# One four-bank score tile and one exp per chunk in a sliding-window attention kernel

## The chip, the cores and the metric

The kernel runs on one core of one Trainium2 chip. The metric is device time in microseconds (us). An execution mostly repeats within 0.3% to 1%.

Names of engines: PE is the tensor engine (PEld its weight loads), ACT the scalar engine, DVE the vector engine, POOL the general-purpose engine, SP the engine that issues most transfers. PSUM has eight banks of 512 fp32 columns per partition (the Trainium skill, "PSUM — Partial Sum Buffer", Specifications), and the pools of this kernel take exactly eight.

## The reference, cut to what matters

```python
x = A_x                                          # 2048 tokens, 512 features, bf16
h = layernorm(x) * (1 + ca) + sa
q, k, v = split(h @ wqkv)                        # 32 heads of 16
scores = q @ k.T * 16**-0.5                      # causal, window of 256
x = x + ga * (softmax(masked scores) @ v @ wo)
h = layernorm(x) * (1 + cb) + sb
x = x + gb * token_mlp(layernorm(h))             # over tokens: 2048 -> 1792, gelu, -> 2048
```

The modulation vectors `ga`, `ca` and so on come from a small product with `w_mod`.

## The kernel before

The queries are worked off in 4 groups of 512 tokens, each with 4 head groups of 8 heads. A head group of query group 0 has four chunks and every other has five, 76 in all. A chunk is up to 512 score columns for each of four row tiles (32 rows of the array each, two heads to a row tile). It goes PE (scores) to ACT (exp) to DVE (two mask multiplications) to PE (attention-value, AV, and the sum of the exps). Projections of the next query group, output projections, layer norms and the first part of the MLP are cut into slices and emitted between chunks as background.

Four of the eight banks hold scores, as two tiles of two banks. Two banks serve the background (`ps_d`) and two the AV results (`ps_o`), so all eight are taken.

```python
ps_d = ...tile_pool(name="ps_d", bufs=2, space=PSUM)
ps_s = ...tile_pool(name="ps_s", bufs=2, space=PSUM)    # two tiles of two banks
ps_o = ...tile_pool(name="ps_o", bufs=1, space=PSUM)

def emit_scores(G, g8, ch):
    tiles = []
    for a in range(2):
        pss = ps_s.tile([P, 2, D], F32, name="pss")
        for kb, qs, nq, col in ch:
            ...
            for jj in range(2):
                rows = slice(32 * (2 * a + jj), 32 * (2 * a + jj) + 32)
                nc.tensor.matmul(pss[:, jj, col : col + KB * nq], ..., tile_position=(32 * (2 * a + jj), 0))
        tiles.append(pss)
    return tiles

def emit_exp_mask(tiles, ch, masks):
    et = epool.tile([P, 4, D], BF, name="et")
    for a in range(2):
        nc.scalar.activation(out=et[:, 2 * a : 2 * a + 2, lo:D], in_=tiles[a][:, :, lo:D], func=ACT.Exp, scale=SCORE_SCALE)
    for col, stride, m0, mn in masks:            # two multiplications on DVE
        ...

for i, (u, ci, ch, mk) in enumerate(steps):
    ...
    et = emit_exp_mask(tiles, ch, mk)            # exp and masks of chunk i
    tiles = emit_scores(... steps[i + 1] ...)    # scores of chunk i + 1
    pend.append((u, ci, ch, et))
    ...                                          # slices of background
    emit_av(...)                                 # AV of chunk i - 1; after the last chunk Ln, Exp, normalise
```

After attention the score banks serve the MLP as accumulators, two output blocks to a tile. The framework tracks a PSUM tile as a whole.

The softmax here doesn't subtract the row's maximum and nothing guards it: scores larger than these inputs give would overflow.

## Time and profile before

| | before |
|---|---|
| time, median | 318.3 us |
| profiled span | 316.3 us |
| first exp starts / last exp ends | 23.3 / 225.4 us |
| that stretch | 202.1 us, 2.66 us a chunk |
| after the last exp | 90.9 us |

The page of the kernel before gives busy time and share of the span by engine (first two rows), and the chain that ended last by engine (third):

```profile
PE 266.9 (84%) x3271; PEld 130.4 (41%) x3313; DVE 229.4 (73%) x517; ACT 184.2 (58%) x241; POOL 33.8 (11%) x68
...
PE 45%; ACT 20%; DVE 19%; issue 5%; another core or an unknown queue 0%
```

No engine reads as full, and the chain runs through three of them.

The groups of instructions by form (line, engine, operation, out<-in, shape, count, then busy us and mean ns, then idle time before them and what ended it) give the two lengths of an exp:

```profile
L417 ACT ACTIVATE et<-pss 128x1024 bf16<-128x1024 f32 x144 | 140.7, 1033 | 26.8 <-PE pss L403 26.4
...
L417 ACT ACTIVATE et<-pss 128x768 bf16<-128x768 f32 x8 | 6.2, 819 | 6.5 <-PE pss L403 6.5
```

The timeline of ACT (start, length, what) holds this row:

```profile
89.84 5.81 ACT L417 ACTIVATE et<-pss 128x1024 bf16<-128x1024 f32 x6
```

Six exps take 5.81 us, about 0.97 each; where one directly follows another, starts are 0.904 us apart (median of 72). Finally, from the waits of PE (who waited on whom: us in total, times, longest):

```profile
PE pss L403 <- ACT et L417: 9.6, 27, 0.7
...
PE poy L469 <- DVE et L424: 2.4, 1, 2.4
```

Scores wait for an exp a little each time, and AV hardly ever waits for a mask. Three rows of PE's timeline show the usual order of its work here, scores, then a slice of background (`pv`), then AV:

```profile
89.11 0.85 PE L403 MATMUL pss<-QT_1_128,KT_1_136 32*128 32x128 bf16 x12
89.89 1.06 PE L326 MATMUL pv<-wqkv,h1T 128*64 128x256 bf16 x16
90.89 0.27 PE L469 MATMUL pox<-et,VT_144 128*32 128x192 bf16 x4
```

### The profile page before, as it was taken

How to read it: one execution, taken by the hardware profiler on the slowest of the kernel's cores; microseconds unless marked ns; L12 is line 12 of the kernel's file. 1: busy time of each engine (PE TensorE's matmuls, PEld its weight loads, DVE VectorE, ACT ScalarE, POOL GpSimd, SP SyncE). 2: the span in 40 equal slices, each digit the busy share in tenths (PEclk: the TensorE clock that was granted, in tenths of full speed). 3: DMA queues.
4: the chain of work that ended last, by engine and by line, in shares of the span. 5: the costliest groups of instructions: out<-in, count | busy, mean ns of one | idle time of the engine just before them, and what ended most of it. 6: DMA issues, size and time to landing. Idle time of an engine off the chain costs nothing.

```text
span 316.3 us, 7673 instructions
## 1 busy us (share of the span) xinstructions
PE 266.9 (84%) x3271; PEld 130.4 (41%) x3313; DVE 229.4 (73%) x517; ACT 184.2 (58%) x241; POOL 33.8 (11%) x68
## 2 busy tenths in 40 slices
PE   0488898988895989988699898899992999999994
PEld 0343345434453534445244444444441444444441
DVE  7989998656999865999774498945389376455353
ACT  2016887799895799899496699977511254000000
POOL 8501301121020032020041000000000000000000
PEclk9999999999998699999699999999999899999999
DMA  7993007900000000000001300033310895101111
GB/s 215 335 349 34 3 2 200 264 6 2 2 3 2 2 2 2 2 2 3 1 2 51 86 2 2 0 105 99 93 42 0 289 414 227 52 34 50 50 35 51
DMA packets 31435, 24.63 MB, mean 78 GB/s; under 512 B 6056, under 2 KB 29608, under 8 KB 31400
## 3 DMA queue, kind: packets, MB, share of 16 engines
q1 hardware_dynamic: 30336, 23.08, 23.9%
q10 hardware_dynamic: 1064, 1.05, 1.1%
q8 instruction: 26, 0.43, 0.6%
q14 instruction: 9, 0.07, 0.1%
HBM read 22.03 MB, written 2.10 MB: 76 GB/s over the span
## 4 chain that ended last, share of the span: by engine, by line
PE 45%; ACT 20%; DVE 19%; issue 5%; another core or an unknown queue 0%
ACT et L417 15%; PE pu L446 6%; PE pss L403 5%; DVE st L243 4%; PE pox L469 4%; PE poy L469 2%; ACT lz L481 2%; PE pu_4759 L653 2%; PE pu_4917 L653 2%; PE pu_4798 L653 2%; PE pu_4956 L653 2%; PE pq L291 2%; PE pv L326 2%; DVE et L424 2%; ACT lz L480 1%
## 5 line engine op out<-in xcount | busy, mean ns | idle before, releaser
L417 ACT ACTIVATE et<-pss 128x1024 bf16<-128x1024 f32 (+1 forms) x152 | 146.8, 1022 | 33.3 <-PE pss L403 32.9
L469 PE MATMUL poy<-et,ones_bd 128*32 128x128 bf16 (+4 forms) x768 | 42.4, 257 | 2.6 <-DVE et L424 2.4
L424 DVE TENSOR_TENSOR et<-et,maskt 128x256 bf16<-128x256 bf16 (+2 forms) x104 | 35.4, 360 | 12.3 <-ACT et L417 12.0
L429 DVE TENSOR_TENSOR et<-et,maskt 128x512 bf16<-128x512 bf16 x48 | 21.2, 442 | 18.0 <-ACT et L417 17.4
L653 PEld LDWEIGHTS <-w2r 128*128 128x128 bf16 x224 | 21.9, 98 | 26.5
L469 PE MATMUL pox<-et,VT_143 128*32 128x320 bf16 (+4 forms) x352 | 19.4, 259 | 3.5 <-DVE OT_1_151 L482 1.2
L469 PEld LDWEIGHTS <-ones_bd 128*32 128x32 bf16 x768 | 19.5, 98 | 6.7 <-issue 4.5
L291 PE MATMUL pq<-h1T,wqkv 128*128 128x512 bf16 x58 | 17.1, 401 | 3.0 <-DVE VT_143 L336 1.3
L326 PE MATMUL pv<-wqkv,h1T 128*64 128x256 bf16 x256 | 18.6, 285 | 0.6 <-DVE KT_0_131 L306 0.5
L300 PE MATMUL pk<-h1T,wqkv 128*128 128x512 bf16 x57 | 16.5, 397 | 2.2 <-DVE kb L312 0.9
L621 ACT ACTIVATE g<-a,b1FM 128x512 bf16<-128x512 f32 x14 | 9.6, 716 | 12.4 <-DVE a L619 12.4
L326 PEld LDWEIGHTS <-h1T 128*64 128x64 bf16 x256 | 13.3, 113 | 4.7 <-issue 2.6
L469 PEld LDWEIGHTS <-VT_143 128*32 128x32 bf16 x352 | 9.1, 96 | 13.5 <-issue 12.9
L246 ACT ACTIVATE rs<-mv,eps_t 128x4 f32<-128x4 f32 x12 | 3.7, 307 | 18.7 <-DVE mv L244 18.7
L312 DVE CAST kb<-pk 128x512 bf16<-128x512 f32 x15 | 10.3, 688 | 5.6 <-issue 2.5
L469 PE MATMUL pox<-et,VT_144 128*32 128x320 bf16 (+4 forms) x208 | 11.1, 268 | 2.5 <-DVE OT_1_147 L482 2.1
L480 ACT ACTIVATE lz<-poy 128x512 f32<-128x512 f32 x16 | 9.7, 608 | 4.4 <-PE poy L469 4.3
L469 PE MATMUL pox<-et,VT_145 128*32 128x320 bf16 (+4 forms) x208 | 11.1, 261 | 1.0 <-DVE OT_2_152 L482 0.5
L336 DVE CAST VT_143<-pv 64x512 bf16<-64x512 f32 x16 | 11.0, 687 | 0.2
L481 ACT ACTIVATE lz<-lz 128x512 f32<-128x512 f32 x16 | 10.4, 649 | 0.0
L300 PEld LDWEIGHTS <-wqkv 128*128 128x128 bf16 x64 | 5.5, 101 | 9.5 <-issue 4.7
L291 PEld LDWEIGHTS <-wqkv 128*128 128x128 bf16 x64 | 5.5, 100 | 8.5 <-issue 3.6
(647 smaller groups left out, 547.3 us busy)
## 6 DMA issues: line engine op xcount, KB each, us to landing
w2r<-in_B_w_dram SPq DMA_DIRECT2D x14, 512.0 KB, 10.0
wmod<-in_w_mod_dram SPq DMA_DIRECT2D x4, 512.0 KB, 6.9
out_dram<-otile SPq DMA_DIRECT2D x16, 128.0 KB, 1.7
wmod<-in_w_mod_dram ACTq DMA_DIRECT2D x2, 512.0 KB, 5.7
wqkv<-in_A_wqkv_dram SPq DMA_DIRECT2D x2, 384.0 KB, 6.2
wqkv<-in_A_wqkv_dram SPq DMA_DIRECT2D x1, 512.0 KB, 6.6
wod<-in_A_wo_dram SPq DMA_DIRECT2D x1, 512.0 KB, 8.6
w1p_1241<-in_B_w_dram SPq DMA_DIRECT2D x1, 512.0 KB, 4.0
```

Source lines behind the costliest of these rows:

```text
L291: nc.tensor.matmul(pq[:], lhsT=wqkv[:, dc, g8 * P : (g8 + 1) * P], rhs=h1T[:, dc, :], start=(dc == 0), stop=(dc == ND - 1),)
L300: nc.tensor.matmul(pk[:], lhsT=wqkv[:, dc, D + g8 * P : D + (g8 + 1) * P], rhs=h1T[:, dc, :], start=(dc == 0), stop=(dc == ND - 1),)
L326: nc.tensor.matmul(pv[KB * par : KB * (par + 1), i, :].rearrange("p (a d) -> p a d", d=DH), lhsT=h1T[:, dc, tok], rhs=wv[:, dc, par, :, :] ...
L403: nc.tensor.matmul(pss[:, jj, col : col + KB * nq], lhsT=KT[r][g8][rows, kbi, :, :], rhs=QT[G % 2][g8][rows, KB * qs : KB * (qs + nq)], st ...
L417: nc.scalar.activation(out=et[:, 2 * a : 2 * a + 2, lo:D], in_=tiles[a][:, :, lo:D], func=ACT.Exp, scale=SCORE_SCALE,)
L424: nc.vector.tensor_tensor(out=dst, in0=dst, in1=msk.to_broadcast([P, 4, KB * mn]), op=ALU.mult,)
L429: nc.vector.tensor_tensor(out=dst, in0=dst, in1=maskt[:, m0 : m0 + 2, :].unsqueeze(1).to_broadcast([P, 4, 2, KB]), op=ALU.mult,)
L446: nc.tensor.matmul(pu[:], lhsT=w1s(sc, fc), rhs=hb[sc][:], start=(sc == 0), stop=(sc == 7),)
L469: nc.tensor.matmul(dst[32 * j : 32 * j + 32, KB * qs : KB * (qs + nq)], lhsT=VT[r][:, kbi, 4 * u.g8 + j, :] if isv else ones_bd[:], rhs=et ...
L480: nc.scalar.activation(out=lz[:], in_=u.y[:], func=ACT.Ln)
L481: nc.scalar.activation(out=lz[:], in_=lz[:], func=ACT.Exp, scale=-1.0)
L653: nc.tensor.matmul(ftiles[100 + t], lhsT=w2r[:, fc, t * P : (t + 1) * P], rhs=guT[fc][:], start=(fc == 0), stop=(fc == NF - 1), skip_group ...
```

## The change

The intent is to halve the number of exps and of score groups, saving their fixed costs. The score tile becomes one tile of four banks. As there are only four banks for it, there is one buffer instead of two. The MLP uses the same pool, so its accumulators follow: four output blocks to one tile.

```diff
-    ps_s = ctx.enter_context(tc.tile_pool(name="ps_s", bufs=2, space=PSUM))
+    ps_s = ctx.enter_context(tc.tile_pool(name="ps_s", bufs=1, space=PSUM))
...
-        for a in range(2):
-            pss = ps_s.tile([P, 2, D], F32, name="pss")
-            for kb, qs, nq, col in ch:
-                for jj in range(2):
+        pss = ps_s.tile([P, 4, D], F32, name="pss")
+        for kb, qs, nq, col in ch:
+            for j in range(4):
                     (the same matmul, row tile j)
...
-        for a in range(2):
-            nc.scalar.activation(
-                out=et[:, 2 * a : 2 * a + 2, lo:D], in_=tiles[a][:, :, lo:D], func=ACT.Exp, scale=SCORE_SCALE,
-            )
+        nc.scalar.activation(
+            out=et[:, :, lo:D], in_=tiles[:, :, lo:D], func=ACT.Exp, scale=SCORE_SCALE,
+        )
...
-    f_tiles([("s", [0, 1]), ("s", [2, 3]), ("x", [4]), ("y", [5])])
+    f_tiles([("s", [0, 1, 2, 3]), ("x", [4]), ("y", [5])])
...
-    homes = [("d", 1), ("d", 1), ("s", 2), ("s", 2), ("x", 1), ("y", 1)]
+    homes = [("d", 1), ("d", 1), ("x", 1), ("y", 1), ("s", 4)]
```

More of the change, by code (lines that the diff above doesn't have):

```diff
@@ L395, in emit_scores @@
     def emit_scores(G, g8, ch):
-        tiles = []
-        for a in range(2):
-            pss = ps_s.tile([P, 2, D], F32, name="pss")
-            for kb, qs, nq, col in ch:
-                r, kbi = ring(kb, G)
-                for jj in range(2):
-                    rows = slice(32 * (2 * a + jj), 32 * (2 * a + jj) + 32)
-                    nc.tensor.matmul(
-                        pss[:, jj, col : col + KB * nq],
-                        lhsT=KT[r][g8][rows, kbi, :, :],
-                        rhs=QT[G % 2][g8][rows, KB * qs : KB * (qs + nq)],
-                        start=True, stop=True, tile_position=(32 * (2 * a + jj), 0),
-                        skip_group_check=True,
-                    )
-            tiles.append(pss)
-        return tiles
+        pss = ps_s.tile([P, 4, D], F32, name="pss")
+        for kb, qs, nq, col in ch:
+            r, kbi = ring(kb, G)
+            for j in range(4):
+                rows = slice(32 * j, 32 * j + 32)
+                nc.tensor.matmul(
+                    pss[:, j, col : col + KB * nq],
+                    lhsT=KT[r][g8][rows, kbi, :, :],
+                    rhs=QT[G % 2][g8][rows, KB * qs : KB * (qs + nq)],
+                    start=True, stop=True, tile_position=(32 * j, 0),
+                    skip_group_check=True,
+                )
+        return pss
     def emit_exp_mask(tiles, ch, masks):
@@ L415, in emit_exp_mask @@
         et = epool.tile([P, 4, D], BF, name="et")
-        for a in range(2):
-            nc.scalar.activation(
-                out=et[:, 2 * a : 2 * a + 2, lo:D], in_=tiles[a][:, :, lo:D], func=ACT.Exp, scale=SCORE_SCALE,
-            )
+        nc.scalar.activation(
+            out=et[:, :, lo:D], in_=tiles[:, :, lo:D], func=ACT.Exp, scale=SCORE_SCALE,
+        )
         for col, stride, m0, mn in masks:
@@ L584, in f_tiles @@
             if kind == "s":
-                t = ps_s.tile([P, 2, D], F32, name="pu2", tag="pss")
+                t = ps_s.tile([P, 4, D], F32, name="pu2", tag="pss")
                 for i, fc in enumerate(group):
@@ L627 @@
         gelu(fc)
-    for kind, group in (("d", [6]), ("d", [7]), ("s", [8, 9]), ("s", [10, 11]), ("x", [12]), ("y", [13])):
+    for kind, group in (("d", [6]), ("d", [7]), ("s", [8, 9, 10, 11]), ("x", [12]), ("y", [13])):
         f_tiles([(kind, group)])
```

## The prediction

> **What bounds the kernel now.** The page: PE busy 84% of 316.3 us, DVE 73%, ACT 58%. Exps run from 23.3 to 225.4 us (timeline), 2.66 us a chunk; there the change acts. By windows, ACT is busy 36.5 of 45.5 us in head group 0 (DVE 39.0), 44.2 of 50.5 in group 1, 45.3 of 54.7 in group 2, 42.6 of 52.0 in group 3 (PE 46.9). No engine is full; the chain of waits gives PE 45%, ACT 20%, DVE 19%. Two score tiles let the next scores fill one while the exp reads the other: six exps run back to back from 89.84 to 95.65 us (timeline).
>
> **Removed.** 76 of 152 exps. A 1024-column exp takes 1.02 us, but back to back their starts are 0.904 us apart. At 0.836 ns per column (groups by form: 819 ns for 768 columns, 1033 for 1024) a 2048-column exp should take 1.88 us (estimate), 4 us less in all. The Trainium skill ("Perfetto Trace Analysis", Optimizing Scalar/DVE Operations) says grouping helps a saturated engine; this trace shows the fixed cost mostly overlapped.
>
> Four row tiles now stand next to each other, not two and two. A chunk's twelve take 0.6 us now, a half group of six 0.40 us. Twelve on four row tiles should take 0.43 us (estimate): 0.17 us of PE per chunk saved, 13 us in all, off the path.
>
> **Added.** One four-bank buffer: the next scores wait for the whole exp, the next exp for all scores. Timeline: exp end to first score 0.05 us, scores 0.43, last score to exp 0.04: 0.52 us with ACT idle. "Perfetto Trace Analysis" (Matmuls) advises rotating banks so that evacuation overlaps the next matmuls; those six exps show that it works here. A chunk's floor becomes 1.88 + 0.52 = 2.40 us instead of 1.81.
>
> **On the critical path.** Twenty chunks of a group: 48 us, plus four normalisation pairs (Ln, Exp; 0.5 us each beyond the gap) and small work: 51 us before any lateness, against 50.5, 54.7 and 52 measured with it. In the built order one attention-value group (AV) and a slice of background, about 1.63 us of PE, stand between two score groups: nearly an exp. AV waits for masks (0.43 + 0.28 us after the exp), so slack is 0.1 to 0.3 us, and late DVE work now delays scores and exp at once. I expect 3 to 8 us more in groups 1, 2 and 3 each, 1 to 3 in group 0 (DVE-bound), 0 to 1 in the MLP tail.
>
> **Prediction: 330 us, range 318 to 344.** Faster by over 2%: 0.06; within 2%: 0.24; slower by over 2%: 0.70.
>
> **What would show each step.**
> - 76 exps, mean about 1.88 us; ACT busy within 4 us of 184.
> - No exp directly after another: ACT idle ended by score matmuls rises from 33 us in 28 waits to over 45 in some 60.
> - Scores wait for the exp far more than 27 times.
> - The exp stretch grows from 202 us to 210 to 218.
> - Time after the last exp changes under 2 us.
>
> **What would make it wrong.** If PE and DVE lateness sets today's 2.66 us rather than ACT, saved PE time and an evener order could hide the 0.52 us: within 2%, or faster. If AV waits long for masks, every chunk slips and it passes 344. If four row tiles don't overlap: +13 us.

## More of the kernel before

The program order is not the issue order: the framework's scheduler orders each engine's queue from its own estimate of when inputs are ready.

The windows of exactly the exp stretch (columns: window, length, then busy time and instruction count of PE, PEld, DVE, ACT, POOL, then granted clock, DMA share, GB/s):

```profile
23.33:225.41 202.08, 176.27 (x2755) 87.70 (x2789) 156.92 (x378) 168.42 (x215) 22.80 (x30) 0.97 0.15 37
```

PE is busy 176.3 of 202.1 us here, so it is idle for 25.8.

Counted over the exp stretch, PE goes from scores to background 69 times and from scores straight to AV 40 times.

## The result, and the profile after

| | before | after |
|---|---|---|
| time, median | 318.31 us | 332.75 us |
| ratio, 95% interval | | 1.0475, 1.042 to 1.053 |
| profiled span | 316.3 us | 329.7 us |
| first exp starts | 23.3 us | 24.7 us |
| exp stretch | 202.1 us | 210.9 us |
| after the last exp | 90.9 us | 94.1 us |

The result is right against the reference. The 13.4 us of span come as 1.3 before the first exp, 8.9 in the exp stretch and 3.2 in the tail. The page after:

```profile
PE 256.8 (78%) x3269; PEld 125.8 (38%) x3313; DVE 227.3 (69%) x517; ACT 182.6 (55%) x165; POOL 34.8 (11%) x68
...
PE 37%; DVE 35%; ACT 15%; DMA 8%; issue 3%; SPq 1%; another core or an unknown queue 0%; DVEq 0%; ACTq 0%
...
L413 ACT ACTIVATE et<-pss 128x2048 bf16<-128x2048 f32 (+1 forms) x76 | 140.6, 1851 | 35.2 <-PE pss L401 34.6
```

There are half as many exps, and together they save little: ACT's busy time on the page falls by 1.6 us. PE does less work (10.1 us less busy) and yet the kernel is longer. The windows of the exp stretch say where:

```profile
24.65:235.59 210.94, 166.55 (x2778) 83.98 (x2815) 154.85 (x376) 166.20 (x137) 23.86 (x30) 0.98 0.15 37
```

PE busy fell from 176.3 to 166.6 us, but PE idle (length less busy) rose from 25.8 to 44.4. The waits of PE after name what it waited for:

```profile
PE pox L465 <- DVE et L425: 13.3, 21, 1.3
...
PE pss L401 <- ACT et L413: 7.0, 14, 1.3
PE pox L465 <- DVE et L420: 3.7, 10, 0.5
PE poy L465 <- DVE et L420: 3.5, 7, 0.9
```

AV now waits 20.5 us for masks (13.3 + 3.7 + 3.5), against 2.4 before. Waits for the exp are no more than before. Six rows of the timeline show the step, ACT's rows first and then PE's (the bracket is the idle time before, and what ended it):

```profile
92.97 1.88 ACT L413 ACTIVATE et<-pss 128x2048 bf16<-128x2048 f32 x1 [0.50 <-PE pss L401]
96.18 1.88 ACT L413 ACTIVATE et<-pss 128x2048 bf16<-128x2048 f32 x1 [1.33 <-PE pss L401]
```

```profile
92.52 0.40 PE L401 MATMUL pss<-QT_1_128,KT_1_136 32*128 32x192 bf16 x8
...
93.81 0.27 PE L465 MATMUL pox<-et,VT_144 128*32 128x192 bf16 x4 [0.88 <-DVE et L425]
...
94.39 1.40 PE L326 MATMUL pv<-wqkv,h1T 128*64 128x256 bf16 x18
95.73 0.40 PE L401 MATMUL pss<-QT_1_128,KT_1_136 32*128 32x128 bf16 x12
```

The exp that started at 92.97 ends at 94.85. Its successor's scores could start then. But PE stood waiting 0.88 us for the masks of the chunk before, does its AV and a slice of background, and reaches the scores only at 95.73. The next exp starts at 96.18, after 1.33 us of ACT idle. The gap before the exp at 92.97 was a turn without lateness, 0.50 us.

The order of PE's work has changed too: AV follows the scores at once, and the background comes after it. PE now goes from scores to background 15 times and straight to AV 62 times (69 and 40 before). The edit did not ask for this. It is the order that the framework's scheduler built for one buffer, and it leaves the masks less time. Why the scheduler chose it is not known.

Counted over all 75 gaps between exps, the medians of the parts are: scores 0.399 us from first start to last end, last score to exp 0.052 us, and in 35 gaps the scores start within 0.07 us of the exp's end. In the other 40 they are late, by 19.0 us in all.

### The profile page after: what moved, and what is told of

Read it like the earlier page. It is cut to its first block, busy times and chain, and to the rows that moved or that the text cites. A ratio compares the mean times of both kernels' runs of the same rounds, so it can differ in the third digit from the quotient of the medians. Undisturbed runs are those within 1.5% of the kernel's fastest.

```text
span 329.7 us, 7582 instructions
## 1 busy us (share of the span) xinstructions
PE 256.8 (78%) x3269; PEld 125.8 (38%) x3313; DVE 227.3 (69%) x517; ACT 182.6 (55%) x165; POOL 34.8 (11%) x68
## 4 chain that ended last, share of the span: by engine, by line
PE 37%; DVE 35%; ACT 15%; DMA 8%; issue 3%; SPq 1%; another core or an unknown queue 0%; DVEq 0%; ACTq 0%
ACT et L413 11%; DVE st L243 6%; PE pu_4802 L649 4%; PE pu_4645 L649 4%; PE pu L442 4%; DVE et L420 4%; PE pss L401 3%; PE pox L465 3%; DVE et L425 3%; PE pu_4257 L592 2%; DMA x_73<-in_A_x_dram 2%; DMA wqkv<-in_A_wqkv_dram 2%; PE pu_4484 L592 2%; DMA b2b<-in_B_b_dram 2%; DVE VT_143 L336 2%
## 5 line engine op out<-in xcount | busy, mean ns | idle before, releaser
L413 ACT ACTIVATE et<-pss 128x2048 bf16<-128x2048 f32 (+1 forms) x76 | 140.6, 1851 | 35.2 <-PE pss L401 34.6
L420 DVE TENSOR_TENSOR et<-et,maskt 128x256 bf16<-128x256 bf16 (+2 forms) x104 | 32.9, 338 | 9.9 <-ACT et L413 9.6
L465 PE MATMUL pox<-et,VT_143 128*32 128x320 bf16 (+4 forms) x352 | 18.4, 255 | 9.3 <-DVE et L425 4.3
L465 PEld LDWEIGHTS <-ones_bd 128*32 128x32 bf16 x768 | 20.4, 97 | 8.3 <-DVE et L420 7.3
L326 PE MATMUL pv<-wqkv,h1T 128*64 128x256 bf16 x256 | 19.3, 277 | 1.1 <-DVE KT_0_131 L306 0.5
L465 PEld LDWEIGHTS <-VT_143 128*32 128x32 bf16 x352 | 11.4, 94 | 17.6 <-issue 16.5
L465 PE MATMUL pox<-et,VT_144 128*32 128x320 bf16 (+4 forms) x208 | 11.3, 264 | 7.3 <-DVE et L425 4.6
L465 PE MATMUL pox<-et,VT_145 128*32 128x320 bf16 (+4 forms) x208 | 10.7, 256 | 6.6 <-DVE et L425 4.3
L312 DVE CAST kb<-pk 128x512 bf16<-128x512 f32 x15 | 10.2, 682 | 5.8 <-PE pk L300 3.0
L465 PEld LDWEIGHTS <-VT_144 128*32 128x32 bf16 x208 | 7.2, 98 | 11.8 <-issue 11.0
L465 PEld LDWEIGHTS <-VT_145 128*32 128x32 bf16 x208 | 6.9, 96 | 10.8 <-issue 9.9
L477 ACT ACTIVATE lz<-lz 128x512 f32<-128x512 f32 x16 | 10.1, 631 | 0.4
```

The source lines that it names most:

```text
L326: nc.tensor.matmul(pv[KB * par : KB * (par + 1), i, :].rearrange("p (a d) -> p a d", d=DH), lhsT=h1T[:, dc, tok], rhs=wv[:, dc, par, :, :] ...
L413: nc.scalar.activation(out=et[:, :, lo:D], in_=tiles[:, :, lo:D], func=ACT.Exp, scale=SCORE_SCALE,)
L420: nc.vector.tensor_tensor(out=dst, in0=dst, in1=msk.to_broadcast([P, 4, KB * mn]), op=ALU.mult,)
L465: nc.tensor.matmul(dst[32 * j : 32 * j + 32, KB * qs : KB * (qs + nq)], lhsT=VT[r][:, kbi, 4 * u.g8 + j, :] if isv else ones_bd[:], rhs=et ...
```

## The experiments

Throttled time will be needed for reading them: the trace records stretches in which PE is granted half its clock. In the exp stretch they come to 13.7 us before and 10.2 us after, so they don't explain the result.

### MLP accumulators as before

The changed attention, with its score pool closed before the MLP and two two-bank tiles opened in its place.

```diff
+    sst.close()
+    ps_s = ctx.enter_context(tc.tile_pool(name="ps_m", bufs=2, space=PSUM))
-                t = ps_s.tile([P, 4, D], F32, name="pu2", tag="pss")
+                t = ps_s.tile([P, 2, D], F32, name="pu2", tag="pss")
     (and the three lists of blocks as before)
```

> The changed kernel, but with the MLP part of the kernel before (two two-bank tiles instead of one four-bank tile; attention is built in the same order). Theory: after the last exp the changed kernel takes 94.1 us against 90.9, because the last four output blocks share one tile and each block's first matmul waits for the vector engine's read of the block before it (about 0.8 us, three times at the end). Then this run loses 2.5 to 3.5 us: about 329.5 us, with 90.5 to 92 us after the last exp, and a start-to-end exp stretch of 211 us as in the changed kernel. Rival: the longer tail comes from the later end of attention itself; then it stays at 332 to 334 us with a tail of 94 us.

Measured: 328.82 us, ratio to before 1.033 (1.025 to 1.041). The stretch stayed at 211.6 us, and the tail fell to 90.0 us. The chain of the changed kernel shows the cause (start, length, what):

```profile
310.24 3.04 PE pu_4802 L649 x14
313.28 0.03 issue
313.30 0.76 DVE o_4817 L632
314.06 0.04 issue
314.10 3.19 PE pu_4802 L649 x14
```

Fourteen matmuls fill one bank of the four-bank tile. The next fourteen go to another bank, but as it is the same tile they wait until DVE has read the first: 0.8 us, three times in the last four blocks. With the accumulators as before, the end of the chain is unbroken PE work:

```profile
299.81 7.12 PE pu L652 x33
306.93 0.05 issue
306.99 10.74 PE pu L652 x49
317.73 0.05 issue
317.78 4.49 PE pu L652 x20
```

The two-bank tiles have the same wait. There the scheduler put matmuls of another tile into it; with the four-bank tile last there was no other. So the 3.2 us by which the tail had grown belong to the MLP and not to attention: undoing the MLP part took 4.1 us off the tail, 3.1 off the span and 3.9 off the median (different rounds). The theory held, with slightly more gained than the 2.5 to 3.5 us it gave.

### Scores in half order

```diff
-        for kb, qs, nq, col in ch:
-            for j in range(4):
+        for a in range(2):
+            for kb, qs, nq, col in ch:
+                for j in (2 * a, 2 * a + 1):
```

> The changed kernel, but the twelve score matmuls of a chunk stand in the order of the kernel before: all pieces of row tiles 0 and 1, then all of 2 and 3. Nothing else differs in the built order. Theory (scores and exp take turns, so the score time is on the critical path): a score group takes about 0.60 us instead of 0.40, and some 60 of 75 gaps between exps grow by 0.2 us: plus 9 to 13 us, 341 to 346 us. Rival (late vector work and the attention-value matmuls set the chunk time, the turn-taking is hidden): plus less than 4 us.

Measured: 332.32 us, ratio 1.044 (1.034 to 1.054): no slower than the changed kernel. The edit did not do what it was to do: the score group took 0.412 us (median) instead of 0.399. A group built as 192, 192, 320, 320 columns on row tiles 0 and 1, then the same on 2 and 3, started in the trace with all four of 192 at 120.846, .852, .862 and .865 us, and the four of 320 from .928. The later row tiles do not wait for the earlier ones' second piece. So side by side or not makes 0.01 us here, not the 0.17 that the prediction counted on. The run says nothing on whether score time is on the path.

In fact the kernel before also does twelve matmuls in 0.41 us when both its buffers are free and the clock is full. The prediction's 0.6 us fits the first of these two rows of its timeline. No exp ran during that row, but it lies in a throttled stretch (100.81 to 107.64 us), so it is half clock and not a cost of the order:

```profile
107.18 0.61 PE L403 MATMUL pss<-QT_3_130,KT_3_134 32*128 32x192 bf16 x12
...
223.03 0.41 PE L403 MATMUL pss<-QT_3_130,KT_3_134 32*128 32x128 bf16 x12
```

### Two exps from the one tile

```diff
-        nc.scalar.activation(out=et[:, :, lo:D], in_=tiles[:, :, lo:D], ...)
+        for a in range(2):
+            nc.scalar.activation(out=et[:, 2 * a : 2 * a + 2, lo:D], in_=tiles[:, 2 * a : 2 * a + 2, lo:D], ...)
```

> The changed kernel with its one four-bank tile and its one score group, but two exps of 1024 columns again. Theory (what costs is the single buffer, and merging the exp is worth 0.05 us a chunk): plus 1 to 5 us, 333 to 338 us, still with scores waiting for the second exp. Rival (the long exp instruction itself costs, as it holds back masks or the scores for 1.88 us): back towards the kernel before, 318 to 325 us.

Measured: 339.85 us, ratio 1.065 (1.056 to 1.074). Splitting the exp again does not bring the time back; it is 7 us slower than the changed kernel, more than the 1 to 5 expected. Part of the excess may be clock: 27.3 us of its stretch are throttled, against 10.2, and PE is busy about 5 us longer. PE idle is 46.6 us, near the changed kernel's 44.4. The long exp instruction is not the cause.

### One exp with two buffers, and its control

Both give wrong results on purpose (they passed the comparison all the same, presumably because the attention branch weighs little in the output; that was not checked). All twelve score matmuls of a chunk go to row tiles 0 and 1, into one two-bank tile, of which there are two. The first reads the tile twice over in one 2048-column exp; the control reads it with two exps of 1024. MLP as before.

```diff
-                    rows = slice(32 * (2 * a + jj), 32 * (2 * a + jj) + 32)
+                    rows = slice(32 * jj, 32 * jj + 32)
...
+            in_=tiles[:, :, lo:D].unsqueeze(1).to_broadcast([P, 2, 2, D - lo])      # one exp
```

```diff
+        for a in range(2):                                                          # the control
+            nc.scalar.activation(out=et[:, 2 * a : 2 * a + 2, lo:D], in_=tiles[:, :, lo:D], ...)
```

> Wrong results on purpose. The merged 2048-column exp with double buffering kept: the twelve score matmuls go to row tiles 0 and 1 twice, into a two-bank tile that the exp reads twice over (a repeated dimension), and there are two such tiles as in the kernel before; MLP as before. Theory (the single buffer costs): the idle time of the scalar engine before exps that score matmuls end goes back to a few long waits, many exps directly follow each other about 1.77 us apart, and the time is 310 to 322 us. Rival (the merged exp is the cause): 328 us or more although there are two buffers.

> Wrong results on purpose, the control of the run with a merged exp and two buffers (321.5 us): the same twice-read two-bank tiles and twelve score matmuls on two row tiles, but two exps of 1024 columns again. If merging the exp is worth its 0.05 us or less per chunk, this run takes 320 to 326 us. If merging by itself costs (the long instruction), it takes 318 us or less.

Measured: 321.48 us with one exp (ratio 1.010, 1.001 to 1.019), 319.22 us with two (1.005, 0.999 to 1.011). The windows of the stretch, first one exp, then two:

```profile
24.71:227.30 202.59, 171.61 (x2735) 92.36 (x2771) 154.40 (x376) 163.87 (x139) 23.16 (x30) 0.96 0.14 35
```

```profile
25.71:225.44 199.73, 174.37 (x2770) 91.25 (x2771) 153.63 (x376) 167.65 (x215) 23.15 (x30) 0.97 0.14 36
```

With two buffers and a merged exp the stretch is back to 202.6 us. PE idles 31.0 us with one exp and 25.4 with two. Merging alone therefore shows no gain; it may cost 2 us (the intervals overlap, so this is not settled). One buffer against two, with the same exp and the same MLP, is the run with the MLP as before against this one: 328.8 against 321.5 us, 211.6 against 202.6 us of stretch, 44.5 against 31.0 us of PE idle. And this one has a handicap, as its scores use two row tiles and take 0.61 us. But the two runs differ in PE's order as well: with two buffers the scheduler again puts background after the scores (58 times, straight to AV 22 times). The pair shows what one buffer costs together with the order that the scheduler builds for it, not the buffer alone. The control came out at 319 us, 0.8 below the range for "merging is worth its 0.05 us or less", and above the 318 for "merging costs".

### Scores twice

Each score matmul is issued twice into the same place, so results stay right. This lengthens the score time, which the half order had failed to do.

```diff
-        for kb, qs, nq, col in ch:
+        for kb, qs, nq, col in ch * 2:
```

> The changed kernel with every score matmul issued twice into the same place (same result), because the run with the old order left the score time at 0.41 us and so did not lengthen it. Theory (scores and exp take turns on one buffer): a score group takes about 0.61 us instead of 0.40, the gap between exps without other scalar work in it grows from about 0.50 to 0.71 us, and some 60 chunks pay it: plus 9 to 16 us, 342 to 349 us. Rival (the turns are hidden behind late vector work): plus less than 5 us.

> The control: the kernel before with every score matmul issued twice. With two buffers the extra 0.21 us a chunk should be done during the other exp. Theory: plus 0 to 7 us (318 to 325 us), clearly less than the changed kernel pays. Rival (the tensor engine's time counts alike in both kernels): the same 9 to 16 us in both.

Measured: changed kernel 363.43 us (ratio 1.142, 1.136 to 1.148), kernel before 354.96 us (1.116, 1.110 to 1.122). Both lie far above what either theory said, and the control contradicts mine. Windows of the stretch of the control and of the changed kernel:

```profile
23.70:259.74 236.04, 209.31 (x3537) 114.20 (x3538) 156.65 (x375) 172.16 (x215) 24.66 (x30) 0.90 0.13 32
```

```profile
31.11:267.44 236.33, 185.05 (x3554) 98.01 (x3554) 148.34 (x364) 166.62 (x135) 23.91 (x28) 0.93 0.12 33
```

In the kernel before, PE's busy time grew by 33.0 us and the stretch by 33.9; PE's idle time hardly moved (25.8 to 26.7). Extra PE time was not hidden behind the other exp at all. That points to PE as the limit of this stretch, though it reads 87% busy there. In the changed kernel busy time grew by 18.5 us and the stretch by 25.4, as a score group took 0.621 us and lateness grew from 19.0 to 29.3 us. The sizes are not clean: throttled time in the stretch rose to 47.8 and 34.1 us, which lengthens PE's busy time as well, and the changed kernel's first exp came 6.5 us later for a reason not pursued. The direction that survives is that PE's time is on the path in both kernels.

### No masks

Wrong results on purpose: the mask loop runs over nothing.

```diff
-        for col, stride, m0, mn in masks:
+        for col, stride, m0, mn in ():
```

> Wrong results on purpose: the kernel before without the 152 mask multiplications, so 56 us less of vector work and no wait of the attention-value matmuls for masks. Expected 295 to 310 us.

> Wrong results on purpose: the changed kernel without the mask multiplications. Theory (a floor of about 2.4 us a chunk from turn-taking, to which lateness of 19 us is added): the late starts of score groups after the exp shrink, but the floor stays, so it gains less than the kernel before: 316 to 325 us, and the distance between the two kernels grows from 14 to over 17 us. Rival (the single buffer costs only because it lets late masks through to scores and exp): the distance shrinks to under 8 us.

Measured: 314.25 us for the kernel before (ratio 0.987, 0.981 to 0.992), slower than expected, and 324.10 for the changed one (1.018, 1.011 to 1.024). The distance between the two fell from 14.4 to 9.9 us: between the two theories, and it did not grow as mine said. In the stretch it fell from 8.9 to 4.6 us (198.3 and 202.9 us). The waits of PE in the changed kernel without masks:

```profile
PE pss L401 <- ACT et L413: 16.5, 34, 1.4
...
PE pox L465 <- ACT et L413: 1.1, 1, 1.1
```

The 20.5 us for masks are gone, and scores wait for the exp 16.5 us instead of 7.0. Lateness fell from 19.0 to 9.6 us. So part of the penalty really was masks, and part only changed its name: when PE no longer waits for the mask it arrives sooner at the occupied score tile.

### Pinned order

Three runs pin PE's matmuls in the attention loop to the order in which the program emits them: scores, background, AV of an older chunk.

```diff
+    nc.tensor.matmul = lambda *a, **k: tc.keep_in_program_order(mm0(*a, **k))
+    nc.tensor.transpose = lambda *a, **k: tc.keep_in_program_order(tr0(*a, **k))
```

The second of them also does AV for two chunks at a time and background every other chunk:

```diff
-        while bg and credit >= 1.0:
+        while bg and credit >= 1.0 and i % 2 == 0:
-        while len(pend) > (1 if i + 1 < len(steps) else 0):
+        while (i % 2 or i + 1 == len(steps)) and len(pend) > (1 if i + 1 < len(steps) else 0):
```

> The kernel before (two buffers) with the tensor engine's matmuls in the attention loop pinned to the order in which the program emits them: scores of the next chunk, background, attention-value of the chunk before last. Changes between score, attention-value and full-array matmuls fall from 296 to 200 in the built order, and attention-value has a chunk more for its masks. Theory (in the kernel before the tensor engine limits, and each change of tiling costs about 0.1 us, as a matmul after a change starts 0.07 us before the end of the one before it and without a change 0.16 us): minus 5 to 12 us, 306 to 314 us. Rival (the strict order makes the engine wait for background inputs): 318 us or more.

> As the run with the program order, but attention-value comes for two chunks at a time and background every other chunk: 140 changes of tiling instead of 296. Theory: minus 8 to 18 us against the kernel before, 300 to 311 us. Rival: the larger blocks hold up the scores and idle the scalar engine: slower than the run with the program order.

> The changed kernel (one buffer) with the same pinned order, results right. Theory (of the changed kernel's penalty about half is late score groups behind attention-value matmuls that wait for masks): with background between the scores and the attention-value of an older chunk, the lateness of score groups after the exp falls from 19 us to under 9 us, and the run takes 316 to 326 us; it stays slower than the kernel before with the same order by at least 4 us, because exp and scores still take turns. Rival (lateness has another cause): 330 us or more.

Measured: 344.20, 363.31 and 349.11 us (ratios 1.082, 1.137 and 1.097). All three missed. The first exp came at 31.7 to 33.3 us instead of 23.3 or 24.7, as the pin also held the first scores behind all projections of the first query group, a fault of my edit. The stretch had 61 to 75 us of throttled time. Whether fewer changes of tiling would save PE time is left open; these runs can't tell.

Two readings of the third are still of use. AV has a chunk more for its masks there, and its list of waits holds none for masks. In place of them stands this row:

```profile
PE pss L519 <- ACT et L413: 35.1, 40, 2.3
```

With one buffer the wait moved to the exp. In the same order with two buffers the wait of scores for the exp was 11.6 us.

The second reading compares the first run (two buffers) with the third (one). They are the only pair with the same order of PE's work, and they have 61.4 us of throttled time each. The windows of their stretches, two buffers first:

```profile
33.30:251.77 218.47, 177.82 (x2746) 83.94 (x2746) 147.83 (x358) 166.93 (x210) 20.14 (x27) 0.86 0.12 32
```

```profile
32.24:250.50 218.26, 167.20 (x2746) 82.03 (x2746) 148.62 (x359) 166.02 (x134) 20.80 (x27) 0.86 0.12 32
```

The stretches are equally long: PE is busy 10.6 us less with one buffer and idle 10.4 us more. The spans differ by 4.4 us, and that comes from the tail (90.7 and 96.4 us). So in this order the turns cost the stretch no more than the shorter PE work gave back. At half clock for over a quarter of the time this does not carry over to the kernels at full clock, but it forbids calling the buffer alone the cause.

No version that I ran beats the kernel before with right results.

### All runs side by side

All numbers are of the exp stretch, in us. "Mask + exp" adds PE's waits for masks and for exps; "to background / AV" counts how often PE went from scores to each.

| run | score buffers | length | PE busy | PE idle | mask + exp | throttled | to background / AV |
|---|---|---|---|---|---|---|---|
| before | 2 | 202.1 | 176.3 | 25.8 | 12.0 | 13.7 | 69 / 40 |
| two exps, two buffers | 2 | 199.7 | 174.4 | 25.4 | 4.7 | 13.7 | 56 / 22 |
| one exp, two buffers | 2 | 202.6 | 171.6 | 31.0 | 7.2 | 17.1 | 58 / 22 |
| before, no masks | 2 | 198.3 | 179.1 | 19.2 | 8.4 | 10.2 | 74 / 37 |
| before, scores twice | 2 | 236.0 | 209.3 | 26.7 | 10.9 | 47.8 | 57 / 21 |
| after | 1 | 210.9 | 166.6 | 44.4 | 27.5 | 10.2 | 15 / 62 |
| after, MLP as before | 1 | 211.6 | 167.1 | 44.5 | 27.7 | 10.2 | 15 / 62 |
| after, half order | 1 | 211.4 | 166.9 | 44.4 | 29.1 | 10.2 | 15 / 62 |
| after, two exps | 1 | 218.5 | 171.9 | 46.6 | 26.2 | 27.3 | 8 / 69 |
| after, no masks | 1 | 202.9 | 168.3 | 34.6 | 16.5 | 13.7 | 9 / 68 |
| after, scores twice | 1 | 236.3 | 185.1 | 51.3 | 29.7 | 34.1 | 3 / 72 |
| before, pinned | 2 | 218.5 | 177.8 | 40.7 | 11.6 | 61.4 | 55 / 19 |
| before, pinned pairs | 2 | 236.1 | 179.1 | 57.1 | 21.8 | 75.1 | 31 / 37 |
| after, pinned | 1 | 218.3 | 167.2 | 51.1 | 35.1 | 61.4 | 55 / 19 |

Among the runs in the scheduler's own order the buffers sort PE's waits, and the number of exps does not. Kernels with two buffers make PE wait 5 to 12 us for masks and exps, and every kernel with one buffer and masks 26 to 30 us. In the same runs the last column is sorted as well: with two buffers background mostly follows the scores, with one buffer AV does. Buffer and order changed together everywhere but in the pinned runs. "Mask + exp" is not all of the idle time: the two-exps and one-exp runs with two buffers also wait 15.7 and 16.1 us for the normalisation to free the AV tile, the kernels before and after 5.7 and 5.8.

## Why the prediction was right or wrong

The time (332.75 us against 330, range 318 to 344), the direction and the mechanism (scores and exp take turns, and late masks then delay both) were right; several terms of the sum were not. The nearness of the time is partly luck. The prediction's terms add up to 10 to 28 us, so its 330 lies at the low end of its own sum. Its terms for attention come to 10 us or more (its list of tests says 8 to 16), and the stretch lost 8.9; for the tail and the start the sum held 1 us at most, and they lost 4.5.

- **The merged exp: right.** 76 exps of 1.877 us (median) against 1.88. The exps of the kernel before, 0.904 us apart and 1.023 long, had hidden most of their fixed cost behind each other already. The Trainium skill has the formula 186 ns + 0.833 ns per column for an exp without pointer operands ("ScalarE: Activation LUTs", What ACT_TABLE_LOAD costs), which gives an estimate of 1.892 us; the trace is within 1%. ACT's busy time fell by 1.6 us, within the 4 given.
- **The turn of 0.52 us: right.** 0.05 + 0.40 + 0.05 us. With the exp merged in both, two buffers took the stretch from 211.6 to 202.6 us, so going to one buffer is shown as the cause, together with the order that the scheduler then builds. How much the turn costs by itself is not shown: in the pinned order it cost the stretch nothing (218.5 and 218.3 us).
- **"0.17 us of PE per chunk saved, 13 us in all, off the path": size near, both reasons wrong.** PE's busy time in the stretch fell by 9.7 us. But the half order showed that placing four row tiles side by side is not what saves it (0.412 against 0.399 us). More likely it is that a chunk's two half groups no longer run apart, each after its own wait; no run shows this alone. And it was not off the path: with the scores twice, each us of PE time in the kernel before lengthened the stretch by about one (part of both is half clock).
- **"No engine is full": misread, as far as the scores twice can tell.** PE at 87% of the stretch was the engine that counted. The change made PE's work 9.7 us shorter and its idle time 18.6 us longer; the sum is the 8.9 us of the stretch.
- **Lateness: right kind, wrong row.** I named late masks as the danger, and AV waits for masks went from 2.4 to 20.5 us. I also said that the scores would wait for the exp far more than 27 times; the list of waits shows 14. PE mostly stood at AV instead, which the new order puts straight behind the scores, so the cost is entered under masks. Idle time of ACT ended by scores was 34.6 us in 49 waits, not over 45 in some 60.
- **By query group (the prediction calls them head groups in places): mixed.** From the first exp of one to the first of the next, plus 1.3, 4.3, minus 1.0 and plus 4.4 us; I had said 3 to 8 in each of the last three. In group 2 of the kernel before two chunks start over 5 us before the next (6.9 us, with throttled clock, and 5.1 us); in the changed kernel none there takes more than 3.6.
- **Tail: wrong.** I said 0 to 1 us (under 2 as a test); it was 3.2. The last output blocks share a tile and each waits for DVE's read of the one before; undoing the MLP part removed it.
- **Start:** plus 1.3 us before the first exp was not in the sum. The timelines show why: the first exp of the kernel before needs four score matmuls, the last of which started at 22.99 us; the merged exp needs eight, the last of which started at 24.31, with projections in between.

## What to carry to other kernels

Halving the count of an instruction whose fixed cost already hides behind its neighbour gains almost nothing, and paying for it with the second buffer makes producer and consumer take turns. A scheduler may answer the lost buffer with another order of work, so compare the order of the busiest engine before and after, not only its waits: here buffer and order changed together, and only a run with pinned order could part them. Look at idle time of the engine that limits, not at its share on the page: test it by adding work to it and seeing whether the time follows. And when a wait is removed, look where it reappears before counting it as gained; a tile that several accumulations share also makes them wait for each other's readers.

## What the Trainium skill lacked or had wrong

- "PSUM — Partial Sum Buffer" (Engine vs sequencer instructions) says that matmuls start and complete in program order. With different row tiles they started out of it: two 192-column matmuls that the built program (scores in half order) has behind two of 320 on other row tiles started 0.063 to 0.066 us before these (120.862 and .865 against .928 us).
- "TensorEngine Tiling (Array Packing)" (Key Properties) says that changing the tiling mode drains the engine, without a cost. In the kernel before the next matmul started 0.067 to 0.070 us before the end of the one before it at 213 of the 284 changes in the stretch, and 0.164 us (median) before it among full-array matmuls without a change: an estimate of 0.1 us a change. The profile models the ends of matmuls, so this is rough. Whether avoiding them pays is not shown.
- "TensorE: Matmul & The Clock Gate" (What's actually happening) gives half clock after at least one idle window of about 3.4 us. Throttled stretches here last multiples of 3.4 us, which agrees. But in the attention part of the kernel before they began after 8 us in which PE was busy for 64% and 68% with no idle time longer than 2.4 us, and slowed variants had up to 75 us of them; at what load they begin no page tells.
- No page says how waits on a PSUM tile of several banks are placed. Here the first matmul into another bank of the same tile waited for DVE's 0.76 us read of the first, 0.8 us each time.
